# A new placing of stage 1, of the DMA transpositions and of the vector work in a hand-ordered FFT filter and MLP kernel

## The chip, the core and the metric

The kernel runs on one core of a Trainium2 chip. The metric is the device time of one execution in microseconds, as the median of several runs. TensorE (PE) multiplies matrices, with PEld its weight loads; VectorE (DVE), ScalarE (ACT) and GpSimd (POOL) work on elements; SyncE (SP) and POOL issue DMAs. Each engine works through its own instructions in the order in which the program gives them, and waits on semaphores for the others.

## The reference

Eight batches of 3008 tokens with 256 features go through a Fourier filter along the tokens, and every token then through two matrix products with a leaky ReLU between them.

```python
X = np.fft.rfft(x, axis=1)                    # x: (8, 3008, 256)
Y = X * (filt_r + 1j * filt_i)[None, :, :]    # filters: (1505, 256)
y = np.fft.irfft(Y, n=3008, axis=1).astype(np.float32)
h = y.reshape(24064, 256) @ w_in              # w_in: (256, 2048)
out = np.maximum(0.01 * h, h) @ w_out         # w_out: (2048, 256)
```

## The kernel before

**The filter** is a Fourier transform of 3008 = 94 x 32 points, done as small matrix products in fp16. For batches 1 to 7 it has four stages, cut into groups:

- Stage 1 (`s1_group`, 16 groups of a batch, matmuls L265): transforms of length 94. The result is copied out of PSUM into `turn_in` (L266, by ScalarE or VectorE). When all 16 groups are there, six DMA transpositions (`t1_load`, L273, issued by SP) turn `turn_in` into the quads `z1[0]` to `z1[5]`. There is one `turn_in`: the next batch's stage 1 may write it only after the last of the six has read it.
- Stage 2 (`s2_group`, 12 groups, L311): transforms of length 32, then the product with the filter. VectorE makes p2 (L320) and p1 (L323) out of PSUM, SP moves the halves of p2 across partitions with two shift copies (L321, L322), and POOL adds p1 and the shifted p3 to `y` (L326). In the even groups of batch 1 VectorE makes p3 itself (L317, L318), with no shift copies.
- Stage 3 (`sa_group`, 12 groups, L333): the inverse transform of length 32; ScalarE copies the result out (L335), and SP stores it to DRAM (L337). SP loads it back in another order as `z2` (`t2_load`, L281).
- Stage 4 (`sb_group`, 16 groups, L358): the inverse transform of length 94, copied to the ring `yt` (L347), which holds six chunks of 512 tokens.

Batch 0 goes through a separate sequence of steps, written out by hand, at the start.

**The MLP** runs over 47 chunks of 512 tokens. `moe1` (L524) multiplies by `w_in`, 16 tiles to a chunk in pairs into two wide PSUM banks, and ScalarE applies the leaky ReLU (L527, 8 times a chunk) into `gt_c`. The second product (L597) uses, from chunk 3 on, a two-by-two scheme with seven products in place of eight (m1 to m7, among them `last_product`), for which VectorE makes four sums (`act_sums`, L563) and combines the results (L625, L633, L641, L647, L650, L661). SP stores the rows (L583).

**The order** is written by a planner in this file. `at(time, f)` puts the emission of some instructions on a heap, and the heap's order is the program's order on every engine. The times are in units of their own: `SL = 8` units are one chunk. `moe1`, the products and the sums have fixed places in each chunk (`SUMS` for the four sums). The groups of the filter get their places from `PLANS`: for each of batches 1, 2, 3 and 4 (later batches repeat the last row, 47 units on) it has the start and the step of stage 1, the start and the step of stage 2, the lag of stage 3 behind stage 2, the start and the step of stage 4, and the offset and the step of the loads of the next batch's x. No two groups stand closer than `GAP = 0.6` units. A loop over a queue then moves a group back until what it needs has been placed:

- `load_time` places a batch's transpositions `LEAD[0]` units ahead of its stage 2, at the earliest `TURN` after its last stage-1 group, one every `TURNS`.
- A stage-1 group stands at the earliest some units behind the previous batch's last transposition (the line with `TURNS + 0.3`).
- A stage-2 group stands `TURNED` behind its transposition, a stage-4 group `READ` behind its load of z2; a batch's first z2 loads stand `LANDED` behind the last store of stage 3 at the earliest, else `LEAD[1]` ahead of stage 4. Where a place is pushed back, 0.03 is added.

`AFTER` and the numbers in `y_delay` say how far behind stage 2 the shift copies and the additions are emitted (`AFTER[1]`, `AFTER[2]`, `AFTER[3]`), and how far behind a copy the stores (`AFTER[4]`, `AFTER[5]`). `REST` places six late groups of batch 0's inverse transform.

The groups of the filter share two PSUM banks (pf0, pf1; for the first eight units four). `bank` gives a group the one that the planner holds to be free first; `hold` is how long it counts a bank as taken.

Of the kernel before, what the change touches and what calls it, by code (L numbers as in the profile page):

```python
# [19 lines left out]
N1, N2 = 94, 32  # L20
# [3 lines left out]
NW = 96  # L24
# [54 lines left out]
def kernel(  # L79
# [9 lines left out]
    nc = tc.nc  # L89
    B, N, D = x.shape  # L90
# [6 lines left out]
    NCHUNK = TOK // CH  # L97
# [4 lines left out]
    W0 = 3  # L102
    GAP = 0.6
    EXG = 0
    LANDED = 2.43
    READ = 2.2
    TURN = 0.7
    TURNED = 2.2
    TURNS = 0.9
    SUMS = (0.09, 1.59, 2.35, 4)  # L110
    REST = (5.37, 14.61, 8.86, 10.48, 23.53, 20.72)
    DUE = (3.52, 0.66)
    TWICE = (2.2, 2.35)
    LEAD = (3.3, 7.37)
    AFTER = (0.53, 0.8, 1.33, 3.17, 0.39, 0.52)


    PLANS = (
# [4 lines left out]
    )  # L123

    f2_np, i1_np, small_np, i1t_np = _build_np_constants(N)
# [2 lines left out]
    small_d = nc.inline_tensor(small_np, name="small_const")  # L128
# [5 lines left out]
    small_sb = cpool.tile([P, 5, P], FP16, name="small_sb")  # L134
# [29 lines left out]
    def bank(kind, n, w, hold=0.75):  # L164
        if kind == "ph":
            t = wide[turn[kind] % 2]
            turn[kind] += 1
        else:
            i = min(range(len(single)), key=lambda i: frees[i])
            t, frees[i] = single[i], max(frees[i], clock["now"]) + hold  # L170
        return t[:, : n * w].rearrange("p (n w) -> p n w", n=n)
# [12 lines left out]
    def need(*what):  # L184
        for w in what:
            assert w in issued, w

    def noted(what, f):
        f()
        issued.add(what)  # L190

    def soon(delay, f):
        at(clock["now"] + delay, f)
# [24 lines left out]

    EARLY = 6
    x_early = big[1][:].bitcast(FP32)[:, : EARLY * D].rearrange("p (n d) -> p n d", n=EARLY)  # L220
    nc.sync.dma_start(small_sb[:], small_d.ap())
    nc.sync.dma_start(x_early[:R1], bass.AP(tensor=x.tensor, offset=x.offset, ap=[[N2 * D, R1], [D, EARLY], [1, D]]))
    for n0, nn in ((6, 10), (16, 10), (26, 6)):
        x_load(0, n0, nn)
    for i in range(2):
# [32 lines left out]
    def s1_group(b, g, copy):  # L258
        h, dt = divmod(g, 2)

        def go():
            ps = bank("pf", 4, NW)
            need(("x", b, h if b > 1 else 0), *[("z1", b - 1, 5)] * (b > 1))
            for j in range(4):
                nc.tensor.matmul(ps[:, j, :], x_sb[:, 4 * h + j, ts(dt, P)], fwd1m[:, :NW], start=True, stop=True)  # L265
            copy(turn_in[:, :, dt, :, ds(4 * h, 4)], ps.rearrange("p n (q k) -> p k q n", q=4))  # L266
            issued.add(("s1", b, g))
        return go
# [31 lines left out]
    ys = {}  # L300

    def y_delay(b, g):
        return 1.2 if b == 1 and g % 2 == EXG else AFTER[2] if b > 1 else AFTER[3]

    def s2_group(b, g):
        def go():
            ps = bank("pf", 2, D, 1.75 if b == 1 and g % 2 == EXG else 1.2)
            need(("z1", b, g // 2))
            issued.add(("s2", b, g))
            for j in range(2):  # L310
                nc.tensor.matmul(ps[:, j, :], f2_sb[:, 2 * g + j, :],  # L311
                                 z1[g // 2][:, 2 * (g % 2) + j, :],
                                 start=True, stop=True)
            fa, fb = fa_sb[:, ds(2 * g, 2), :], fb_sb[:, ds(2 * g, 2), :]
            p1, p2, p3 = (scrp.tile([P, 2, D], FP32, tag=f"p{i}", name=f"p{i}_b{b}_g{g}") for i in (1, 2, 3))
            if b == 1 and g % 2 == EXG:
                nc.vector.tensor_tensor(p3[0:64], ps[64:P], fb[64:P], AL.mult)  # L317
                nc.vector.tensor_tensor(p3[64:P], ps[0:64], fb[0:64], AL.mult)  # L318
            else:
                nc.vector.tensor_tensor(p2[:], ps, fb, AL.mult)  # L320
                soon(AFTER[1], lambda: nc.sync.dma_start(p3[0:64], p2[64:P]))  # L321
                soon(AFTER[1], lambda: nc.sync.dma_start(p3[64:P], p2[0:64]))  # L322
            nc.vector.tensor_tensor(p1[:], ps, fa, AL.mult)  # L323
            ys[(b, g)] = y1 = ypp.tile([P, 2, D], FP16, tag="y", name=f"y_b{b}_g{g}")
            soon(y_delay(b, g), lambda: noted(
                ("y", b, g), lambda: nc.gpsimd.tensor_tensor(y1[:], p1[:], p3[:], AL.add)))  # L326
        return go

    def sa_group(b, g):
        def go():  # L330
# [5 lines left out]
            if g % 2:  # L336
                soon(AFTER[4], lambda: noted(("st2", b, h), lambda: nc.sync.dma_start(  # L337
                    dz2[b % 2][ds(4 * h, 4)].rearrange("k p d -> p k d"), st2[h % 3])))
# [11 lines left out]
    def sb_group(b, g, copy):  # L350
        h, dt = g // 2, g % 2

        def go():
            ps = bank("pf", 4, NW)[:, :, :N1]
            need(("z2", b, h), ("i1t",))
            issued.add(("sb", b, g))
            for j in range(4):
                nc.tensor.matmul(ps[:, j, :], z2[h % 3][:, j, ts(dt, P)], i1_sb[:, 4 * h + j, :N1],  # L358
                                 start=True, stop=True)
            quad_copy(b, h, dt, ps, copy)  # L360
        return go
# [154 lines left out]
    def moe1(ci, ct):  # L516
# [9 lines left out]
        if j == 1:  # L526
# [15 lines left out]
    LAST = ((-2.9, 1, 0, NCH), (-1.2, 0, 0, NCH // 2), (-0.5, 2, 0, NCH // 2),  # L542
            (1.05, 0, NCH // 2, NCH // 2), (1.1, 2, NCH // 2, NCH // 2), (1.2, 3, 0, NCH // 2), (3.02, 3, NCH // 2, NCH // 2))
# [69 lines left out]
    def stores(ci, i, of=range(2)):  # L613
        for j in of:
            store(ci, 2 * i + j, rows(ci, i)[:, j, 0:2, :].rearrange("p k d -> p (k d)"))
# [7 lines left out]
    def last_product(ci):  # L623
        def after(po):
            add(rows(ci, 0)[:, :, 1], po, rows(ci, 1)[:, :, 2], AL.add)  # L625
            soon(AFTER[5], lambda: stores(ci, 0))
        return product(ci, lambda: sum_places(ci)[3], b22, after, 3)

    def products(ci):
        a11, a12, a21, a22 = (lambda i=i, j=j: quarter(ci, i, j) for i in range(2) for j in range(2))  # L630

        def after5(po):
            add(rows(ci, 1)[:, :, 1:3], twice(po), part[1], AL.add)  # L633
            soon(AFTER[5], lambda: stores(ci, 1))

# [63 lines left out]
    for g in range(10, 16):  # L699
        at(REST[g - 10], lambda g=g: late_sb(1, g - 8, (act, dve)[g < 12 and g % 2]))  # L700

# [33 lines left out]
    def load_time(stage, b, c):  # L735

        end = stage, b, 15 if stage == 1 else 11
        if (stage, b, c) not in loads:
            if stage == 1:
                if end not in when or (b > 1 and (2, b - 1, 2 * c + 1) not in when):  # L740
                    return None
                t = max(first_use[1, b] - LEAD[0], when[end] + TURN) + TURNS * c
                loads[1, b, c] = t = max(t, place.get((1, c), 0))
            else:
                if end not in when or (c > 2 and (4, b, 2 * c - 5) not in when):
                    return None
                loads[3, b, c] = t = max(first_use[3, b] - LEAD[1], place.get((3, c % 3), 0), when[end] + AFTER[4] + LANDED)
            at(t, (t1_load if stage == 1 else t2_load)(b, c))
# [4 lines left out]
    while queue:  # L753
        time, n, stage, b, g, f = heapq.heappop(queue)
        t = max(time, last + GAP)
        if stage == 3:
            behind = when[2, b, g] + y_delay(b, g) + 0.02 if (2, b, g) in when else None
        else:
            behind = load_time(stage - 1, b, g // 2) if stage != 1 else 0
            if stage == 1 and b > 1:  # L760
                behind = load_time(1, b - 1, 5)
                behind = None if behind is None else behind + TURNS + 0.3
            if stage != 1 and behind is not None:
                behind += TURNED if stage == 2 else READ
        if behind is None or behind + 0.02 > t:
            heapq.heappush(queue, (t + GAP if behind is None else behind + 0.03, n, stage, b, g, f))
            continue
        when[stage, b, g] = last = t
        at(t, f)
        if stage in (2, 4) and g % 2:  # L770
            place[stage - 1, g // 2 % (6 if stage == 2 else 3)] = t + 0.1
        assert stage < 4 or t < SL * (QT * (8 * b + g // 2) // CH), (b, g, t)

    for ci in range(NCHUNK + 1):
        if ci < NCHUNK:
            for ct in range(NCT):
                at(SL * ci + 0.5 * ct, lambda ci=ci, ct=ct: moe1(ci, ct))
        if ci == 0:
            continue
        wino = W0 <= ci - 1  # L780
        items = products(ci - 1) if wino else plain(ci - 1)
        for i, f in enumerate(items):
            at(SL * (ci + i / len(items)) + 0.01, f)
        if wino:
            for time, *what in [(v, i) for i, v in enumerate(SUMS)] if ci < NCHUNK else LAST:
                at(SL * ci + time, lambda ci=ci, what=what: act_sums(ci - 1, *what))
    while work:
        clock["now"], _, f = heapq.heappop(work)
# [31 lines left out]
```

## Time and profile before

| what | value |
|---|---|
| median of 3 runs | 752.54 us (751.26 to 752.71) |
| the profiled execution | 753.01 us, of it 751.0 in the span of the profile |
| PE busy | 734.5 us (98%) |
| ACT busy | 549.2 us (73%) |
| DVE busy | 509.7 us (68%) |
| POOL busy | 166.4 us (22%) |
| matmuls | 8129 |
| mean granted TensorE clock | 0.995 |
| DMA | 98.44 MB, 131 GB/s on average |

The span runs from the first instruction to the end of the last. A row of the profile gives the engine, the line of the kernel, what it writes and reads by the program's names, how often, and the busy time. An idle stretch is given with the engine or the DMA whose signal ended it. `big` is a set of buffers that holds `turn_in`, the quads and the sums, so `DMA big<-big` is a DMA transposition, `dz<-big` a store of stage 3 and `big<-dz` a load of z2.

### The profile page before, as it was taken

Reading aid. Unit: us, or ns where it says so; the run is one execution under the profiler, and the core shown is the slowest. Engines: PE = TensorE matmul, PEld = TensorE weight load, DVE = VectorE, ACT = ScalarE, POOL = GpSimd, SP = SyncE. Lnnn points to the kernel's source line nnn. Section 1 sums busy time; section 2 is a strip of 40 time slices with the busy share of each in tenths; the row PEclk is TensorE's granted clock in tenths of the full one; section 3 lists DMA queues with packets and bytes.
Section 4 is the critical chain, followed back from the end, with each engine's and each line's share of the span. In section 5 each row is a group of like instructions: output and inputs, shape, how many; then the busy total and the mean of one; then the engine's idle time right before and its main releaser. Section 6 shows DMA issues by size and latency. Waiting matters only on the chain.

```text
span 751.0 us, 19526 instructions
## 1 busy us (share of the span) xinstructions
PE 734.5 (98%) x8129; PEld 523.9 (70%) x8129; DVE 509.7 (68%) x696; ACT 549.2 (73%) x763; POOL 166.4 (22%) x171
## 2 busy tenths in 40 slices
PE   8999998999899999999999999999999999999997
PEld 3566675776677777777777777777677777777776
DVE  7878556777566676677666767776577676556466
ACT  4775785787687877787788777877777777776762
POOL 5505401232222312222132331212122210000000
PEclk9999999999999999999999999999999999999999
DMA  9967758676856496465865558343664442212012
GB/s 206 222 106 166 186 127 168 145 177 141 186 135 145 120 176 159 116 146 128 166 150 135 134 140 185 99 130 100 122 174 117 109 111 90 63 54 65 29 46 69
DMA packets 128473, 98.44 MB, mean 131 GB/s; under 512 B 59152, under 2 KB 107152, under 8 KB 128192
## 3 DMA queue, kind: packets, MB, share of 16 engines
q1 hardware_dynamic: 113049, 79.51, 41.2%
q0 software_dynamic: 15056, 17.50, 15.9%
q8 instruction: 63, 1.03, 0.6%
q10 hardware_dynamic: 279, 0.19, 0.1%
q14 instruction: 26, 0.21, 0.1%
HBM read 45.97 MB, written 35.65 MB: 109 GB/s over the span
## 4 chain that ended last, share of the span: by engine, by line
PE 91%; DMA 4%; DVE 2%; ACT 1%; SPq 1%; issue 1%; POOL 0%; ACTq 0%; DVEq 0%; POOLq 0%
PE ph L524 42%; PE po_ps L597 18%; PE pf L597 18%; PE pf L265 3%; PE pf L311 2%; PE pf L333 2%; PE pf L358 2%; DMA big<-big 1%; PE pf L689 1%; PE po_ps L689 1%; DMA f_sb<-fwd_const 1%; DMA x_sb<-in_x_dram 1%; DVE big L563 1%; PE pf L432 0%; ACT yt L347 0%
## 5 line engine op out<-in xcount | busy, mean ns | idle before, releaser
L527 ACT ACTIVATE gt_c<-ph 128x1024 f16<-128x1024 f32 x376 | 384.9, 1024 | 133.0 <-PE ph L524 124.2
L524 PE MATMUL ph<-yt,w_in_sb 128*128 128x512 f16 x1504 | 448.8, 380 | 3.4 <-ACT gt_c L527 3.1
L597 PEld LDWEIGHTS <-gt_c 128*128 128x128 f16 x2800 | 201.7, 98 | 99.2 <-issue 1.7
L326 POOL TENSOR_TENSOR y_b_g<-p_b_g,p_b_g 128x512 f16<-128x512 f32 x84 | 116.8, 1392 | 437.1 <-DMA p_b_g<-p_b_g 292.8
L597 PEld LDWEIGHTS <-big 128*128 128x128 f16 x2128 | 151.6, 98 | 66.0 <-issue 0.5
L524 PEld LDWEIGHTS <-w_in_sb 128*128 128x128 f16 x1504 | 118.4, 98 | 9.2 <-issue 3.5
L320 DVE TENSOR_TENSOR p_b_g<-pf,fb_sb 128x512 f32<-128x512 f32 x78 | 53.6, 687 | 33.1 <-PE pf L311 23.5
L597 PE MATMUL po_ps<-wt_sb,gt_c 128*128 128x128 f16 x704 | 69.8, 219 | 0.0
L347 ACT CAST yt<-pf 128x376 f16<-128x376 f32 (+9 forms) x136 | 58.2, 441 | 14.7 <-PE pf L358 11.8
L597 PE MATMUL pf<-w_out_sb,gt_c 128*128 128x128 f16 x720 | 68.5, 221 | 0.0
L597 PE MATMUL pf<-wt_sb,gt_c 128*128 128x128 f16 x688 | 68.1, 219 | 0.0
L597 PE MATMUL pf<-wt_sb,big 128*128 128x128 f16 x704 | 67.9, 219 | 0.0
L597 PE MATMUL po_ps<-wt_sb,big 128*128 128x128 f16 x688 | 65.7, 219 | 0.0
L597 PE MATMUL po_ps<-w_out_sb,gt_c 128*128 128x128 f16 x688 | 65.0, 219 | 0.0
L563 DVE TENSOR_TENSOR big<-gt_c 128x2048 f16<-128x2048 f16 (+1 forms) x46 | 56.8, 1235 | 3.4 <-ACT gt_c L527 3.3
L563 DVE TENSOR_TENSOR big<-big,gt_c 128x2048 f16<-128x2048 f16 (+1 forms) x45 | 57.4, 1275 | 0.1
L323 DVE TENSOR_TENSOR p_b_g<-pf,fa_sb 128x512 f32<-128x512 f32 x84 | 57.2, 681 | 0.2
L563 DVE TENSOR_TENSOR big<-gt_c,big 128x2048 f16<-128x2048 f16 (+1 forms) x45 | 56.9, 1264 | 0.0
L563 DVE TENSOR_TENSOR gt_c<-gt_c 128x2048 f16<-128x2048 f16 x43 | 56.0, 1303 | 0.9
L335 ACT CAST big<-pf 128x512 f16<-128x512 f32 x84 | 49.0, 584 | 10.4 <-PE pf L333 8.2
L266 ACT CAST big<-pf 128x384 f16<-128x384 f32 x90 | 42.8, 476 | 16.5 <-DMA big<-big 8.1
L358 PE MATMUL pf<-i_sb,big 128*128 128x94 f16 x448 | 37.1, 207 | 0.0
(98 smaller groups left out, 644.9 us busy)
## 6 DMA issues: line engine op xcount, KB each, us to landing
p_b_g<-p_b_g SPq DMA_DIRECT2D x156, 128.0 KB
out_dram<-ost_c_h SPq DMA_DIRECT2D x118, 128.0 KB
dz<-big SPq DMA_DIRECT2D x42, 256.0 KB
big<-dz SPq DMA_DIRECT2D x56, 192.0 KB
x_sb<-in_x_dram POOLq DMA_DIRECT2D x40, 192.0 KB, 4.2
x_sb<-in_x_dram POOLq DMA_DIRECT2D x2, 768.0 KB, 8.8
w_in_sb<-in_moe_w_in_dram POOLq DMA_DIRECT2D x1, 1024.0 KB, 12.8
w_out_sb<-in_moe_w_out_dram POOLq DMA_DIRECT2D x1, 1024.0 KB, 13.7
```

The costliest lines, as they stand in the source:

```text
L265: nc.tensor.matmul(ps[:, j, :], x_sb[:, 4 * h + j, ts(dt, P)], fwd1m[:, :NW], start=True, stop=True)
L266: copy(turn_in[:, :, dt, :, ds(4 * h, 4)], ps.rearrange("p n (q k) -> p k q n", q=4))
L320: nc.vector.tensor_tensor(p2[:], ps, fb, AL.mult)
L323: nc.vector.tensor_tensor(p1[:], ps, fa, AL.mult)
L326: ("y", b, g), lambda: nc.gpsimd.tensor_tensor(y1[:], p1[:], p3[:], AL.add)))
L335: nc.scalar.copy(st2[h % 3][:, ds(2 * (g % 2), 2), :], ps)
L347: copy(yt[:, dt, ds(to, 4 * n)].rearrange("p (a c) -> p a c", c=4), v[:, ds(a, n)])
L358: nc.tensor.matmul(ps[:, j, :], z2[h % 3][:, j, ts(dt, P)], i1_sb[:, 4 * h + j, :N1], start=True, stop=True)
L524: nc.tensor.matmul(ph[:, j, :], w_in_sb[:, dt, ts(ct, P)], yt[:, dt, ds(ci * CH % RING, CH)], start=(dt == 0), stop=(dt == NDT - 1))
L527: nc.scalar.activation(gts[ci][:, ds(2 * g, 2), :], ph, AF.Lrelu)
L563: nc.vector.tensor_tensor(*(v[:, ds(c0, n)] for v in (o, i0, i1)), op)
L597: nc.tensor.matmul(of[t], a()[:, c, ts(t, P)], w[:, c, :], start=(c == 0), stop=(c == NCH - 1))
```

## The change

Nothing is computed otherwise; only places in the order and two DMAs at the start are changed.

- The distance of a batch's first stage-1 groups behind the previous batch's last transposition gets a number of its own, `MARGIN`: 3.838 units in place of `TURNS + 0.3` = 1.2.
- Transpositions start 3.9 instead of 3.3 units ahead of stage 2 and stand 1.015 instead of 0.9 apart.
- `PLANS` is changed for all batches, among it stage 1 of batch 1, 3 and 4 and later, the lag of stage 3 in batch 4 and later, and the loads of x.
- The sums of each chunk stand at other places, with a separate list (`SUMS_FIRST`) for chunk 3; the additions (`AFTER`, `y_delay`), the stores and the late groups of batch 0 (`REST`) move.
- Banks count as held for 0.432 units by groups of stages 1 and 4 (before 0.75) and for 0.753 by groups of stage 2 (before 1.2).
- At the start `small_sb` is loaded in two DMAs: its first fifth (`fwd1`) ahead of `x_early`, the rest behind it.

```diff
-    LANDED = 2.43
-    READ = 2.2
-    TURN = 0.7
-    TURNED = 2.2
-    TURNS = 0.9
-    SUMS = (0.09, 1.59, 2.35, 4)
-    REST = (5.37, 14.61, 8.86, 10.48, 23.53, 20.72)
+    LANDED = 2.836
+    READ = 1.712
+    TURN = 0.889
+    TURNED = 2.3
+    TURNS = 1.015
+    MARGIN = 3.838
+    YD = (0.966, 1.75, 0.753, 0.432, 1.2)
+    SUMS_FIRST = (0.018, 2.103, 2.35, 4)
+    SUMS = (0.322, 1.569, 2.418, 4)
+    REST = (5.339, 14.69, 8.396, 11.015, 24.419, 20.72)
...
-    LEAD = (3.3, 7.37)
-    AFTER = (0.53, 0.8, 1.33, 3.17, 0.39, 0.52)
+    LEAD = (3.9, 7.293)
+    AFTER = (0.454, 0.757, 1.245, 2.615, 0.39, 0.731)
...
-        (0.68, 0.31, 12.6, 1.05, 4.3, 38.33, 2.78, 7.78, 1.5),
-        (23.6, 0.8, 42.87, 2.62, 7.4, 85.59, 2.85, 7.0, 2.12),
-        (46.5, 1.6, 77.28, 3.57, 5.62, 130.03, 2.65, 1.5, 2.2),
-        (79.5, 2.2, 119.86, 3.87, 7.04, 177.42, 2.92, 1.5, 2.55),
+        (0.01, 0.254, 12.6, 1.065, 4.3, 35.584, 2.78, 8.122, 1.518),
+        (23.983, 0.737, 42.87, 2.58, 7.4, 85.174, 2.85, 2.756, 2.12),
+        (47.4, 1.5, 77.28, 3.57, 5.62, 130.659, 2.547, 1.5, 1.552),
+        (81.42, 2.0, 119.86, 3.87, 6.302, 177.538, 2.92, 1.5, 2.55),
...
-    nc.sync.dma_start(small_sb[:], small_d.ap())
+    nc.sync.dma_start(small_sb[:, 0], small_d.ap()[:, 0])
     nc.sync.dma_start(x_early[:R1], ...)
+    nc.sync.dma_start(small_sb[:, 1:], small_d.ap()[:, 1:])
...
-            ps = bank("pf", 4, NW)
+            ps = bank("pf", 4, NW, YD[3])
...
-        return 1.2 if b == 1 and g % 2 == EXG else AFTER[2] if b > 1 else AFTER[3]
+        return YD[0] if b == 1 and g % 2 == EXG else AFTER[2] if b > 1 else AFTER[3]
...
-            ps = bank("pf", 2, D, 1.75 if b == 1 and g % 2 == EXG else 1.2)
+            ps = bank("pf", 2, D, YD[1] if b == 1 and g % 2 == EXG else YD[2])
...
-                behind = None if behind is None else behind + TURNS + 0.3
+                behind = None if behind is None else behind + MARGIN
...
-            for time, *what in [(v, i) for i, v in enumerate(SUMS)] if ci < NCHUNK else LAST:
+            for time, *what in [(v, i) for i, v in enumerate(SUMS if ci - 1 > W0 else SUMS_FIRST)] if ci < NCHUNK else LAST:
```

More of the change, by code (lines that the diff above doesn't have):

```diff
@@ L353, in go @@
         def go():
-            ps = bank("pf", 4, NW)[:, :, :N1]
+            ps = bank("pf", 4, NW, YD[3])[:, :, :N1]
             need(("z2", b, h), ("i1t",))
```

## The prediction

> **What bounds the kernel now.** I read the page first, then the list of TensorE's waits, then the order of time around the two longest of them, then the granted clock there, and last the queue of SyncE (SP) that issues the DMA transpositions.
>
> The page says that TensorE is the bound:
>
> ```profile
> span 751.0 us, 19526 instructions
> PE 734.5 (98%) x8129; PEld 523.9 (70%) x8129; DVE 509.7 (68%) x696; ACT 549.2 (73%) x763; POOL 166.4 (22%) x171
> ```
>
> So a change of order alone, which neither adds nor removes a matmul, can only win what TensorE spends idle or at a low clock. TensorE's own waits, longest first (us in total, times, longest):
>
> ```profile
> PE ph L524 <- ACT gt_c L527: 3.1, 1, 3.1
> PE pf L311 <- ACT big L266: 2.7, 1, 2.7
> ...
> PE pf L333 <- DVE p_b_g L323: 0.7, 1, 0.7
> ...
> PE pf L311 <- DMA big<-big: 0.4, 1, 0.4
> ...
> PE pf L265 <- ACT big L335: 0.3, 1, 0.3
> ```
>
> The two long ones are single events, at 126 us and at 196 us. Both have one cause, seen in ScalarE's order of time (start, us, instruction, idle before it):
>
> ```profile
> 127.64 0.48 ACT L266 CAST big<-pf 128x384 f16<-128x384 f32 x1 [4.70 <-DMA big<-big]
> ...
> 197.89 0.48 ACT L266 CAST big<-pf 128x384 f16<-128x384 f32 x1 [3.43 <-DMA big<-big]
> ```
>
> L266 is the eviction of the next batch's first stage-1 group into turn_in. It may not write before the previous batch's last DMA transposition has read turn_in. ScalarE works in order, so the evictions behind it (gt_c, and a yt of the inverse stage) wait too, and TensorE runs out of PSUM banks. The windows show a second loss (PE, PEld, DVE, ACT, POOL busy, then granted clock):
>
> ```profile
> 131.00:132.00 1.00, 1.00 (x10) 0.88 (x9) 1.00 (x2) 0.95 (x1) 0.42 (x1) 0.50 0.85 244
> 132.00:133.00 1.00, 1.00 (x7) 0.45 (x5) 1.00 (x3) 0.08 (x1) 0.00 (x0) 0.50 0.87 90
> ...
> 199.00:200.00 1.00, 1.00 (x7) 0.48 (x5) 0.99 (x2) 0.67 (x1) 0.71 (x1) 0.50 0.95 288
> 200.00:201.00 1.00, 1.00 (x8) 0.72 (x7) 1.00 (x2) 0.37 (x1) 1.00 (x2) 0.50 0.16 46
> ```
>
> After each gap the clock is halved for a while. With the neighbouring microseconds (0.64 and 0.66 at 130 and 133; 0.77 and 0.52 at 198 and 201) the first stretch loses 0.36 + 0.50 + 0.50 + 0.34 = 1.70 us, the second 0.23 + 0.50 + 0.50 + 0.48 = 1.71 us.
>
> Why the transposition was late, in SP's order of time:
>
> ```profile
> 120.77 1.32 SPq L273 DMA_TRANSPOSE big<-big  x1
> 122.20 0.53 SPq L321 DMA_DIRECT2D p_b_g<-p_b_g  x1
> 122.77 0.60 SPq L322 DMA_DIRECT2D p_b_g<-p_b_g  x1
> 123.42 2.26 SPq L273 DMA_TRANSPOSE big<-big  x1
> 125.77 0.53 SPq L281 DMA_DIRECT2D big<-dz  x1
> ```
>
> SP is issue-bound there: one follows the other with no pause, 1.3 us a transposition, 0.5 to 0.8 us a copy or store. The chain of waits puts the landing 4.09 us behind the issue at 123.42, at 127.50.
>
> **The change part by part.** Only the order on each engine counts; a planned place is a sort key. Eight units are one chunk. From 200 to 550 us the trace has 186 evictions L527, 8 to a chunk, so a chunk takes 350 / 186 x 8 = 15.05 us and a unit 1.88 us.
>
> *The margin.* I worked the planner's placing loop through with both sets of numbers. The last transposition of batch 2 stands at 42.87 - 3.3 + 5 x 0.9 = 44.07 before and 42.87 - 3.9 + 5 x 1.015 = 44.05 after. Batch 3's first group stood at 46.50; now 44.05 + 3.838 pushes it to 47.91: 1.41 units or 2.65 us later. Batch 3 to 4: the last transposition at 78.48 and 78.45, the first group at 79.71 (78.48 + 1.2 + 0.03) and 82.32 (78.45 + 3.838 + 0.03): 2.61 units, 4.9 us. For the other batches the margin never binds (7.4 units or more are there). So it acts at exactly the two places of the two stalls.
>
> *First stall.* In SP's new order the first transposition of batch 2 stands before a 0.31 us load, the second before a store, and one z2 load (0.53 us) goes ahead of the last transposition. Adding the rows up (1.33 us a transposition, 0.8 a store, 0.6 a copy) I get it issued near 123.6 again, so it lands at 127.0 to 128.2. TensorE's matmuls for the group, at 123.16 before, come at 123.16 + 2.65 = 125.8; ScalarE has one more gt_c eviction ahead of it and reaches it at 126.7. It waits 0.3 to 1.5 us instead of 4.70. Two wide banks gave 4.70 - 3.15 = 1.55 us of cover before, so TensorE waits 0 to 1 us; I take 0.4. Win: 3.15 + 1.70 - 0.4 = 4.45 us.
>
> *Second stall.* The same sum puts the last transposition of batch 3 at 194.1 (two shift copies now before it) and its landing near 197.3; the eviction comes at 193.40 + 4.9 + 0.33 = 198.6. It no longer waits. Win: 2.70 + 1.71 = 4.41 us. If that cover of 1.3 us were gone, the cost would return in steps up to these 4.41.
>
> [...]
>
> *Third wait, 0.69 us at 172.75.* A stage-3 group (L333) waited for a bank that L323 emptied late, behind VectorE's sums L563 of 2.31 and 1.96 us. Stage-2 group 9 of batch 2 was placed at 68.05, after the sum at 68.00; now it is at 67.71, ahead of it. Win 0.69; bounds 0 and 0.69.
>
> *Small ones.* The 0.38 us at 538 (batch 7's stage 2 waiting for its first transposition) goes: that transposition is 0.6 units or 1.1 us earlier and now ahead of two shift copies. A 0.13 us gap at 79.39 goes, as the late inverse group moves from 0.13 to 0.96 units behind the user of its bank. The 0.35 us at 83.22 is half kept: the group takes another bank, which VectorE empties at 83.27 instead of ScalarE's 83.52. Win together 0.38 + 0.13 + 0.17 = 0.68.
>
> *Lag 7.04 to 6.302 (batches 4 to 7).* Stage 3 comes 0.74 units or 1.39 us sooner after stage 2. Between the end of the addition L326 and the matmul L333 the trace leaves 0.05 us at batch 7's first group (a wait of 0.20 already), 1.68 at batch 4's, 1.9 at batch 6's, 3.1 at batch 5's. Only batch 7's is short, and its shift copies also issue about 1.3 us earlier in the new SP order. Cost 0 to 1.2 us; I take 0.3.
>
> *Additions, sums, banks.* Additions L326 (AFTER, YD) move by up to 0.56 units on POOL, which is 22% busy; sum 0 moves by 0.23 units, still 6.6 units ahead of its product; shorter holds change which of two banks a group takes, but the least reuse distances stay (0.6 and 1.2 units). Queued behind an early addition or an x load on POOL are only other additions. Batch 4's x loads now follow their stage-1 groups by 0.06 to 1 unit; they wait a little, and nothing reads them for 10 units. The z2 loads (LANDED, READ, LEAD) move by half a unit at most against their stage 4; the trace leaves 4.1 us or more between the end of a batch's first load issue and its first L358, so nothing there. Cost -0.3 to +0.8, taken as 0.3 for waits I have not seen.
>
> *Start.* x_early (L222) no longer has 128 KB of small_sb before it. At some 250 GB/s this is 0.5 us, and ScalarE waited 3.64 us for x_early. But the chain then runs over the x_sb loads and the last third of f2_sb (landing at 20.03), whose bytes are unchanged. Stage 1 of batch 1 starts 0.65 units sooner, where its x is just landing (issue 26.44 + 8.8 gives 35.2 to 35.9; needed at 36.0). Bounds -0.4 and +0.6; taken as 0.
>
> Sum: 4.45 + 4.41 + 0.69 + 0.68 - 0.3 - 0.3 = 9.6 us. TensorE is busy without a gap from 200 to 400 us, so what is won earlier stays won. The profiled execution took 753.01 us (span 751.0) and is 0.47 above the median 752.54: profiled 743.4, median 742.9.
>
> **Rivals.**
> *One stall stays or a new one takes its place.* SP's backlog decides: if the last transposition lands 2 us later than summed, ScalarE again holds back gt_c and one gap with its half clock returns, 4.4 us: 747.3. For it: batch 2's six transpositions, planned over 5 x 0.9 units = 8.5 us, were issued from 111.10 to 123.42, 3.9 us behind the plan. Against: the new order spreads the transpositions and starts them sooner. Chance 0.13.
> *The clock loss is a matter of phase.* If the half clock follows such gaps only in some executions, the median gains only the idle times: 752.54 - 9.6 + 3.4 = 746.3. Against: two gaps of two had it. [...] Chance 0.05.
> *Nothing moves.* The eviction waits for something else than the transposition, and the gap moves with it. The releaser in both rows is the transposition, so 0.05; 752.5.
> *Slower: stage 3 now waits for the additions.* In batches 4 to 7 the lag loses 1.39 us. If shift copies land 2.5 us later than now, the first stage-3 group of each of the four waits about 2.7 us and brings the half clock, 4 x (2.7 + 1.7) = 17.6 us, so 752.5 - 9.6 + 17.6 = 760.5. It decides from 2.4 us a batch on, clock included. For it: 0.05 us of slack at batch 7. Against: 1.7 to 3.1 us at the other three. Chance 0.09.
>
> **How the numbers follow.** The forecast, both stalls gone, has 0.68 and gives 742.9; its own range is 740.9 (11.6: all interior gaps, 7.8, the clock, 3.4, and the start's 0.4, at no cost) to 745. The first two rivals are taken into the range: 741 to 748.5, which leaves out no more than 2 in 10. About 0.2% (1.5 us) is what a measurement of this kernel can tell from no change. Faster: 0.68 + 0.13 + 0.05 = 0.86, less 0.01 for cases near 751, 0.85; same 0.06; slower 0.09.
>
> **What would show it.** Right: no wait of TensorE above 1 us after 36 us, granted clock 1.00 in every stretch there, ScalarE's L266 waiting for the transposition under 1.6 us, TensorE's busy time some 3.4 us lower (the half clock's share), the third wait gone. Wrong: a wait of L333 for L326 in batches 4 to 7, or a clock of 0.50 at a new place; a transposition of batch 2 or 3 landing over 2 us later than 127.5 or 197.8 would refute the SP sum.

## The result, and the profile after

The changed kernel takes 741.05 us (median of 4 runs, 740.08 to 741.88), the kernel before, on the same chip, 751.9 us (4 runs, 750.27 to 752.71). The ratio is 0.9862, with a 95% interval of 0.984 to 0.9883: a win of 8.8 to 12.0 us. The forecast was 742.9 in 741 to 748.5, so the median lies at the lower edge of the range. The profiled execution took 741.42 us, 11.6 less than that of before.

The head of the page after:

```profile
span 739.5 us, 19530 instructions
PE 730.3 (99%) x8129; PEld 521.7 (71%) x8129; DVE 510.1 (69%) x696; ACT 550.0 (74%) x763; POOL 169.0 (23%) x171
```

The same 8129 matmuls keep TensorE busy for 4.2 us less; 3.4 us of that is work that no longer runs at half clock (1.70 and 1.71 us), and no run shows what makes up the rest. The other 7.3 us of the span were idle time. In the list of TensorE's waits after (us in total, times, longest) neither of the two long ones, nor the third wait at L333, is left:

```profile
PE po_ps L384 <- DVE one L242: 1.2, 1, 1.2
PE pf L337 <- POOL y_b_g L330: 1.2, 1, 1.2
PE ph L390 <- ACT x_sb L477: 0.5, 1, 0.5
```

L384 and L390 belong to the first microseconds. L337 is stage 3 (L333 before; the new file is four lines longer); its 1.18 us stand at 537.6, at the first stage-3 group of batch 7. ScalarE's first evictions of the next batch's stage 1 (start, us, instruction, idle before it), the rows that waited 4.70 and 3.43 us before:

```profile
125.44 0.48 ACT L270 CAST big<-pf 128x384 f16<-128x384 f32 x1 [0.29 <-DVE ost_c_h L637]
...
191.66 0.48 ACT L270 CAST big<-pf 128x384 f16<-128x384 f32 x1 [0.69 <-DMA big<-big]
```

The first finds the transposition landed, the second waits 0.69 us for it, which the banks cover. The windows around both places (length, then PE, PEld, DVE, ACT, POOL busy, then granted clock, DMA share, GB/s) show a full TensorE at full clock:

```profile
120.00:130.00 10.00, 10.00 (x117) 7.25 (x116) 7.27 (x11) 7.62 (x11) 3.61 (x3) 1.00 0.96 187
...
190.00:200.00 10.00, 10.00 (x121) 7.24 (x119) 7.05 (x10) 8.09 (x14) 2.21 (x3) 1.00 0.73 188
```

SP's order of time after, for the last two transpositions of batch 2:

```profile
117.91 1.32 SPq L277 DMA_TRANSPOSE big<-big  x1
119.34 0.53 SPq L325 DMA_DIRECT2D p_b_g<-p_b_g  x1
119.91 0.60 SPq L326 DMA_DIRECT2D p_b_g<-p_b_g  x1
120.61 0.53 SPq L285 DMA_DIRECT2D big<-dz  x1
121.19 2.20 SPq L277 DMA_TRANSPOSE big<-big  x1
```

One z2 load now goes ahead of the last transposition, as worked out; the queue is still issue-bound.

Where the 11.5 us of span come from is read by setting the same eviction of moe1 (L527, L531 after) in both traces side by side. The changed kernel leads by 0.6 us at 36.8 (time of before), 1.3 at 114.8, 6.3 at 148, 7.2 at 176, 11.9 at 208, 11.75 at 515, 11.3 at 580 and 11.5 at the end. So: 0.6 at the start, 0.7 in small gaps, 5.0 at the first stall, 0.9 at the third wait, 4.7 at the second stall, nothing for 300 us, and 0.4 lost on balance in batch 7.

### The profile page after: what moved, and what is told of

It reads as the page before. It is cut to its first block, busy times and chain, and to the rows that moved or that the text cites. A ratio compares the mean times of both kernels' runs of the same rounds, so it can differ in the third digit from the quotient of the medians.

```text
span 739.5 us, 19530 instructions
## 1 busy us (share of the span) xinstructions
PE 730.3 (99%) x8129; PEld 521.7 (71%) x8129; DVE 510.1 (69%) x696; ACT 550.0 (74%) x763; POOL 169.0 (23%) x171
## 4 chain that ended last, share of the span: by engine, by line
PE 92%; DMA 3%; POOL 1%; ACT 1%; SPq 1%; DVE 1%; issue 0%; POOLq 0%
PE ph L528 43%; PE pf L601 18%; PE po_ps L601 18%; PE pf L362 3%; PE pf L269 2%; PE pf L315 2%; PE pf L337 2%; DMA fa_sb<-in_filt_r_dram 1%; PE pf L693 1%; PE po_ps L693 1%; DMA fa_sb<-in_filt_i_dram 1%; DMA p_b_g<-p_b_g 1%; SPq L277 1%; POOL prod L416 0%; ACT yt L351 0%
## 5 line engine op out<-in xcount | busy, mean ns | idle before, releaser
L531 ACT ACTIVATE gt_c<-ph 128x1024 f16<-128x1024 f32 x376 | 385.5, 1025 | 132.4 <-PE ph L528 125.4
L330 POOL TENSOR_TENSOR y_b_g<-p_b_g,p_b_g 128x512 f16<-128x512 f32 x84 | 119.2, 1420 | 421.1 <-DMA p_b_g<-p_b_g 292.9
L601 PE MATMUL po_ps<-wt_sb,gt_c 128*128 128x128 f16 x704 | 71.8, 219 | 0.0
L270 ACT CAST big<-pf 128x384 f16<-128x384 f32 x90 | 43.0, 479 | 10.9 <-PE pf L269 8.8
```

The source lines that it names most:

```text
L531: nc.scalar.activation(gts[ci][:, ds(2 * g, 2), :], ph, AF.Lrelu)
L601: nc.tensor.matmul(of[t], a()[:, c, ts(t, P)], w[:, c, :], start=(c == 0), stop=(c == NCH - 1))
```

## The experiments

All were run against the kernel before on the same chip (medians of before there 750.3 to 751.3); ratios have 95% intervals. Three questions: is it the distance alone, what does the rest of the change do, and what is the wait in batch 7 worth?

**The distance alone.** Before, with one number changed:

```diff
-                behind = None if behind is None else behind + TURNS + 0.3
+                behind = None if behind is None else behind + 3.838
```

> The kernel before with one number changed: a stage-1 group stands 3.838 units, not TURNS + 0.3 = 1.2, behind the previous batch's last transposition. By the planner's arithmetic this puts the first groups of batches 3 and 4 at 47.94 and 82.35 (before 46.50 and 79.71; in the changed kernel 47.91 and 82.32) and moves little else. Theory A, the two stalls are only a matter of this distance: both gaps (3.15 and 2.70 us) and both half-clock stretches (1.70 us each) go, 751.9 - 9.3 = 742.6 us, TensorE's wait at 172.75 (0.69 us) may stay or go. Theory B, the earlier and wider placed transpositions on SP are needed as well: the first stall stays in part (a gap of 1 to 2 us, perhaps with its half clock), 744.5 to 748 us.

Measured: 745.58 us (744.24 to 746.66), ratio 0.9936 (0.9917 to 0.9956). Both stalls and both half clocks are gone (mean granted clock 0.999 in the profiled execution, 0.995 in before): the evictions wait 1.64 and 0.66 us, and 0.31 us of idle TensorE is left at 129. Yet only about half of the win is there. The time is that of the second theory, but not for its reason: the first stall is gone. New waits stand at the second place, in the list of TensorE's waits:

```profile
PE pf L358 <- DMA big<-dz: 1.6, 1, 1.6
...
PE pf L333 <- POOL y_b_g L326: 0.8, 2, 0.6
```

Stage 3 waits for an addition, stage 4 for a load of z2. Both wait for things that SP issues behind batch 3's transpositions; its order of time:

```profile
183.41 8.02 SPq L273 DMA_TRANSPOSE big<-big  x5
191.53 1.24 SPq L321 DMA_DIRECT2D p_b_g<-p_b_g  x1
192.82 0.58 SPq L322 DMA_DIRECT2D p_b_g<-p_b_g  x1
193.50 0.54 SPq L337 DMA_DIRECT2D dz<-big  x1
...
197.84 1.50 SPq L281 DMA_DIRECT2D big<-dz  x3
```

Five transpositions in one train, then the shift copies that the addition needs, then the store that the z2 load needs. The reading is that they had time to catch up while TensorE stood still for 2.7 us. A new wait in the stall's place is what the prediction's first rival said, though from another queue entry than it named.

**The changed kernel without the distance.** The loads of x keep their places, so only the stage-1 groups of batches 3 to 7 move back:

```diff
-    MARGIN = 3.838
+    MARGIN = 1.2
-        (47.4, 1.5, 77.28, 3.57, 5.62, 130.659, 2.547, 1.5, 1.552),
-        (81.42, 2.0, 119.86, 3.87, 6.302, 177.538, 2.92, 1.5, 2.55),
+        (46.5, 1.5, 77.28, 3.57, 5.62, 130.659, 2.547, 2.4, 1.552),
+        (79.5, 2.0, 119.86, 3.87, 6.302, 177.538, 2.92, 3.42, 2.55),
```

> The changed kernel with the distance alone undone: MARGIN 1.2, stage 1 of batches 3 and 4 starting at 46.5 and 79.5 as before (their x loads keep their absolute places). The first groups then stand at 46.50 and 79.69, while everything else of the change stays. Theory A: both stalls come back, with their half clock: 741.05 + 9.2 = 750 us. Theory B, the new order on SP brings the transpositions earlier: the gaps come back smaller, 1 to 2 us each, 743.5 to 747 us. If neither comes back (741 to 742), the win was in something else.

Measured: 747.74 us (745.11 to 751.13, 12 runs), ratio 0.9973 (0.9953 to 0.9992). This lies between the two theories: the second stall is back in full, the first in part. The list of its waits has

```profile
PE pf L269 <- ACT big L270: 4.0, 2, 2.7
```

with gaps of 1.34 and 0.60 us at 124 to 126 and of 2.69 at 191.5, the latter alone with the half clock (0.50 from 195 to 197; 1.00 from 124 to 128). Against the change's 0.9862, taking the distance away costs 0.0111, or 8.3 us; against its second measurement further down, 0.9892, it costs 0.0081, or 6.1 us. To the kernel before the distance adds 4.8 us (0.0064 x 751). That the distance and the rest need each other is shown by the new waits in the traces; the times alone would not settle it.

**A shorter distance.** Before with 3.0 in place of 3.838, executed once:

```diff
-                behind = None if behind is None else behind + TURNS + 0.3
+                behind = None if behind is None else behind + 3.0
```

> The kernel before with 3.0 units instead of 1.2: batch 4's first group at 81.51 (no wait), batch 3's at 47.10, only 0.6 units or 1.1 us later than before. Theory A, the eviction's wait shrinks by what the group is moved: ScalarE waits some 3.6 us, TensorE some 2.0 us. On the clock: if a gap of 2 us is enough for the half clock, 3.4 us of it follow the gap and the time is 751.9 - 4.4 - 1.1 = 746.4 us; if not, 744.7 us and no stretch under 1.00. Theory B, the gap jumps (other evictions come between): TensorE waits under 1 us and the time is 743 to 744 us.

Measured: 748.08 us, once. Gaps of 1.05 and 0.32 us at 126 to 128, and a new one of 2.52 at 194.2, where L333 waits for the addition. The mean granted clock of 0.998 is worth about one half clock (0.002 x 746 = 1.5 us) and does not tell where it stood. The expectation missed the second place: there the limit is again the shift copies, not the transposition.

**Distance and spacing.** Is it the wider spacing of the transpositions that clears SP's queue? Before, with the distance and

```diff
-    TURNS = 0.9
+    TURNS = 1.015
-    LEAD = (3.3, 7.37)
+    LEAD = (3.9, 7.37)
```

> The kernel before with the distance of 3.838 units and the transpositions placed as in the changed kernel (3.9 instead of 3.3 units ahead of stage 2, 1.015 instead of 0.9 apart). With the distance alone both gaps were gone, but 2.2 us came back at 196 to 202 us: L333 waited 0.60 us for an addition and L358 1.60 us for a z2 load, both queued on SP behind five transpositions in a row. Theory B, that backlog is what the wider spacing takes away: the two waits fall to 0 to 0.7 us together and the time by 1.5 to 2.2 us below the distance alone, ratio 0.990 to 0.992. Theory C, the backlog comes from the shift copies of batch 3, which stay behind the last transposition here and stand ahead of it in the changed kernel: the waits stay at 1.5 to 2.2 us, ratio 0.993 to 0.994.

Measured: 745.41 us, ratio 0.9935 (0.9916 to 0.9953); run again

> The kernel before with distance and spacing once more, as the measure for the swap on the same chip: 745 to 745.5 us, and a wait of L333 for L326 of 1 to 2.5 us near 193 us in its profile.

745.46 us, 0.994 (0.9918 to 0.9961). The same as with the distance alone: the spacing does not clear it. In the first profile nothing is left at the first place and the wait at the second is longer, with a clock of 0.50 from 196 to 198:

```profile
195.65 0.58 PE L333 MATMUL pf<-y_b_g,small_sb 128*128 128x512 f16 x1 [2.28 <-POOL y_b_g L326]
```

In the second profile TensorE waits at two places, 0.95 us at L333 and 2.46 at L358, with no half clock (1.00 from 194 to 205).

**The spacing alone**, the same two numbers at the old distance of 1.2:

> The kernel before with the transpositions placed as in the changed kernel and the distance kept at 1.2 units (first groups of batches 3 and 4 at 46.50 and 79.69, as before). Theory A, the distance is what counts: both gaps stay, the first at 2 to 3.2 us (the last transposition of batch 2 comes 1 us sooner at most), the second at 2.5 to 3 us, ratio 0.996 to 1.000. Theory B, the spacing alone does half of it: ratio 0.992 to 0.995.

Measured: 749.6 us (12 runs), ratio 0.9988 (0.9973 to 1.0003): no difference that can be told. Gaps of 2.29 us at 124.2 and 2.38 at 192.8, both with their half clock (0.50 from 128 to 131, 0.51 from 196 to 199).

**Shift copies ahead of the last transposition.** In the changed kernel two shift copies of batch 3's first stage-2 group stand ahead of the last transposition. This does that alone, on top of distance and spacing:

```diff
-                soon(AFTER[1], lambda: nc.sync.dma_start(p3[0:64], p2[64:P]))
-                soon(AFTER[1], lambda: nc.sync.dma_start(p3[64:P], p2[0:64]))
+                soon(0.55 if (b, g) == (3, 0) else AFTER[1], lambda: nc.sync.dma_start(p3[0:64], p2[64:P]))
+                soon(0.55 if (b, g) == (3, 0) else AFTER[1], lambda: nc.sync.dma_start(p3[64:P], p2[0:64]))
```

> The kernel before with the distance of 3.838 units and the wider spacing (as in the run with both), and one swap on SP: the two shift copies of batch 3's first stage-2 group stand ahead of batch 3's last transposition, where the changed kernel has them, not behind it. No other engine's order differs. Theory C, the late shift copies are what came in place of the second stall (L333 waited 2.28 us for the addition at 193 to 196 us, and the half clock followed): the copies issue 1.2 to 2 us sooner, the wait falls to under 1 us without the half clock, and the last transposition, 1.2 us later, still lands before its eviction is due or holds it up by less than 2 us. Time 742.5 to 743.5, 2 to 3 us under the run with both. Theory D, the wait is that of POOL or of DMA traffic: it stays at 2 us or more and the time does too.

Measured: 746.0 us, ratio 0.994 (0.9921 to 0.996). The wait for the addition falls to 0.14 us, as expected, and the time does not move: L358 now waits 2.16 us for z2. One wait hid the next. (Three of the six executions have a mean granted clock of 0.997 or 0.998, the profiled one 0.999, so the median may hold a half clock that this profile does not show.) SP's order of time there:

```profile
183.41 5.29 SPq L273 DMA_TRANSPOSE big<-big  x3
188.81 0.54 SPq L321 DMA_DIRECT2D p_b_g<-p_b_g  x1
```

Three transpositions take 5.29 us to issue; the changed kernel's row for the same three has 4.02. On POOL a load of x for batch 4 is issued just then, and another one just ahead of the z2 loads that L358 waits for:

```profile
183.46 0.54 POOL L204 DMA_DIRECT2D x_sb<-in_x_dram  x1
...
194.56 0.54 POOL L204 DMA_DIRECT2D x_sb<-in_x_dram  x1
...
196.12 1.60 SPq L281 DMA_DIRECT2D big<-dz  x3
...
200.56 0.34 PE L358 MATMUL pf<-i_sb,big 128*128 128x94 f16 x4 [2.16 <-DMA big<-dz]
```

**That, and batch 4's loads of x out of the way**, at the places of the changed kernel:

```diff
-        (46.5, 1.6, 77.28, 3.57, 5.62, 130.03, 2.65, 1.5, 2.2),
+        (46.5, 1.6, 77.28, 3.57, 5.62, 130.03, 2.65, 2.4, 1.552),
```

> The kernel before with distance, spacing and the swap on SP, and batch 4's x loads 1.552 instead of 2.2 units apart (starting at 48.9 in place of 48.0, the changed kernel's places): the last two, which ran at 183 and 194 us beside the transpositions and the z2 loads, go ahead of the transpositions. The wait left in the run with the swap was L358's for the first z2 load (2.16 us at 198 us). Theory E, DMA traffic beside the transpositions delays the chain behind them (stage-3 store, z2 loads): the wait falls to under 1.2 us and the time by 1 to 2 us (ratio 0.991 to 0.992). Theory F, it is the place of the last stage-3 group of batch 2 and of its store: the wait stays at 1.8 us or more.

Measured: 742.23 us (741.76 to 746.24), ratio 0.9896 (0.9866 to 0.9926). In the profile:

```profile
186.71 4.02 SPq L273 DMA_TRANSPOSE big<-big  x3
...
192.10 2.52 SPq L273 DMA_TRANSPOSE big<-big  x1
...
199.04 1.45 SPq L281 DMA_DIRECT2D big<-dz  x3
...
202.08 0.34 PE L358 MATMUL pf<-i_sb,big 128*128 128x94 f16 x4 [0.95 <-DMA big<-dz]
```

and the wait for z2 is 0.95 us. No load of x is issued between 176.1 and 200 there; in the changed kernel none between 176.8 and 196.6. The ratio falls by 0.0044, some 3.3 us; the two intervals, each against the kernel before on its own chip, overlap by 0.0005. The profiled execution is the slowest of the six, 746.24 us: it had lost 2.8 us by its first moe1 eviction (39.25 against 36.47 in the run with the swap), and its mean granted clock is 0.996, that of the five others 0.999 or 1.000.

What became shorter is not SP's queue. The three transpositions are issued in 4.02 instead of 5.29 us, but the fourth takes 2.52 instead of 1.62, with no load of x near. A transposition of over 2 us stands elsewhere too without such a load (2.26 us at 123.42 in before), so a load that delays SP is not shown. This trace runs 2.75 us behind the other there (the moe1 evictions at 190.87 and 193.62), and the z2 loads are issued 2.92 later, so no sooner. But from their issue to L358 it is 3.04 us here and was 4.44 with a load of x issued 1.56 us ahead. In the two other profiles in which L358 waited over 1 us for z2, a load of x also stood 0.3 to 1 us ahead, and it took 4.19 us (distance alone) and 5.71 (second profile of distance and spacing). So in these traces the z2 loads land later beside a load of x; that is Theory E, but for the part of the transpositions in it.

With distance, spacing, the swap and the x loads the ratio is 0.9896, against 0.9862 and 0.9892 in the two measurements of the whole change. By the medians all other parts together bring 0.3 to 2.6 us, with intervals that overlap; of these parts only the two below were run by themselves.

**Or an earlier stage 3**, in place of the x loads, by batch 2's stage-2 step as in the change:

```diff
-        (23.6, 0.8, 42.87, 2.62, 7.4, 85.59, 2.85, 7.0, 2.12),
+        (23.6, 0.8, 42.87, 2.58, 7.4, 85.59, 2.85, 7.0, 2.12),
```

> The kernel before with distance, spacing and the swap on SP, and batch 2's stage 2 in steps of 2.58 instead of 2.62 units, as in the changed kernel: its last stage-2 group stands at 73.11 instead of 73.71 and its last stage-3 store, which the first z2 loads wait for, at 79.04 instead of 79.48, 0.44 units or 0.83 us sooner. Theory F: L358's wait for the z2 load (2.16 us in the run with the swap) falls by 0.8 us or, with the shift copies of that group now ahead of the second transposition, to 0 to 1.3 us; ratio 0.991 to 0.993. Theory E, traffic: the wait stays near 2 us.

Measured: 745.02 us, ratio 0.992 (0.9892 to 0.9949). The wait for z2 is gone, so an earlier stage 3 removes it too, but 0.70 us at 158.5 and 0.87 us at L333 at 204.1 have come. The 1 us against the run without it lies within the intervals: no verdict on the time.

**The lag.** The changed kernel with the old lag of 7.04 in batches 4 to 7:

```diff
-        (81.42, 2.0, 119.86, 3.87, 6.302, 177.538, 2.92, 1.5, 2.55),
+        (81.42, 2.0, 119.86, 3.87, 7.04, 177.538, 2.92, 1.5, 2.55),
```

> The changed kernel with the lag of stage 3 behind stage 2 in batches 4 to 7 at 7.04 units again instead of 6.302. Theory A, TensorE's one wait left (1.18 us at 537.6, for the addition L326 of batch 7's first group) is the 1.39 us that the shorter lag took away: the wait falls to 0 to 0.2 us and the time to 739.9 to 740.1 us. Theory B, the addition itself is late (it took 2.26 us there instead of 1.27) and the wait stays or moves: 741 us and a wait of about 1 us.

Measured: 742.34 us, ratio 0.9895 (0.9877 to 0.9914). Batch 7's wait falls from 1.18 to 0.20 us, but batch 6 has a new one:

```profile
453.59 0.38 PE L337 MATMUL pf<-y_b_g,small_sb 128*128 128x512 f16 x1 [1.06 <-POOL y_b_g L330]
```

and there are 0.55 and 0.45 us at 192 and 197. The old lag everywhere is no better.

**The old lag in batch 7 alone**, and the change itself once more on the same chip:

```diff
-        plan(b, p[0] + z, p[1], p[2] + z, p[3], p[4], p[5] + z, *p[6:])
+        plan(b, p[0] + z, p[1], p[2] + z, p[3], p[4] + (0.74 if b == 7 else 0), p[5] + z, *p[6:])
```

> The changed kernel with the lag of stage 3 at 7.04 units in batch 7 alone, 6.302 kept in batches 4 to 6. The wait of 1.18 us at batch 7's first group was 1.18 in both kernels with the shorter lag and 0.2 in all four with the longer one. Theory A, it is the lag: 0.2 us there, nothing new elsewhere, 0.9 to 1.0 us less than the changed kernel (740.1 against 741.05, or 0.13%, at the edge of what the times can tell). Theory B, waiting work is only put off: another wait of about 1 us follows within batch 7 and the times are the same.

> The changed kernel once more, on the chip of this call, so that the others of this call can be set beside it: 741 us, ratio 0.985 to 0.988, one wait of TensorE above 1 us (L337 at batch 7's first group, 1.2 us). If the small waits at 190 to 200 us differ from the first profile, where there were none, they are a matter of the single execution.

Measured: 740.4 us (739.93 to 741.97), ratio 0.9876 (0.9856 to 0.9895), against 741.57 (741.43 to 743.23), 0.9892 (0.9873 to 0.9912) for the change. The wait of 1.18 us stands again at 537.7 in the change, and in the other its row in the list of TensorE's waits is

```profile
PE pf L337 <- POOL y_b_g L330: 0.2, 1, 0.2
```

with no gap above 0.2 us from 36 us on. The medians differ by 1.2 us, the size of that wait, but the intervals overlap: the wait is shown, the time only likely. Its median is the lowest of all runs, but its ratio lies within the intervals of both measurements of the change.

## Why the prediction was right, point by point

- **What bounds it.** Right: TensorE's idle time fell by 7.3 us and its busy time by 4.2 (summed: 3.4 from the half clock).
- **The margin binds at two places only.** Right: with 1.2 again gaps come back at these two places and 6.1 to 8.3 us of the win are gone. Put in alone, though, the distance brings 4.8 us and not the 8.9 of the two stalls; see the first rival.
- **First stall, 4.45 us.** Measured 5.0. The sum for SP was off: the last transposition was issued at 121.19, or 122.5 in before's time (1.3 us lead), 1.1 us earlier than the summed 123.6. The eviction no longer waits for it, and the 0.4 us kept for TensorE are not seen.
- **Second stall, 4.41 us.** Measured 4.7, but the cover was mis-sized. The issue was summed at 194.1 and came at 187.16 + 6.95 (the lead there) = 194.1. The landing was put 3.2 us behind it and came at 191.66, 4.5 behind; ScalarE reached the eviction 0.7 us sooner than summed. The cover of 1.3 us became a wait of 0.69, against the forecast that ScalarE would not wait at all. The win came even so because the banks took it, which was not counted on here; with the swap they took 1.97 us at this eviction without a gap.
- **Third wait, 0.69 us.** The wait is gone and the lead grows by 0.9 there.
- **Small ones, 0.68 us.** The lead gained 0.7 before the first stall and the wait for batch 7's first transposition went. No run takes these apart.
- **Lag, 0.3 us of 0 to 1.2.** Mis-sized: the wait came where it was named, at batch 7's first group, at 1.18 us, the upper end. Batch 7 had 0.20 us of wait before, so about 1.0 us is the lag's. A wait of L333 for L326 in batches 4 to 7 stood among the prediction's signs of being wrong, and one wait above 1 us among what a right one would not show: both came, for this one term.
- **Start, 0.** No difference shown. The first L527 stands at 35.2 to 39.3 us in the profiles without the split load of small_sb and at 35.8 to 36.6 with it; one profile's 0.6 us is no more than that spread.
- **Unforeseen waits, 0.3 us.** None above 0.2 us but batch 7's.
- **The sum of 9.6 us** against 10.9 in the medians of the same chip and 11.5 in the spans. Of the 1.9 us more in the spans 0.8 are the two stalls (5.0 + 4.7 for 4.45 + 4.41), 0.6 the start, 0.4 the small gaps before the first stall (0.7 for 0.30), 0.2 the third wait and 0.3 the unforeseen waits that did not come; batch 7 goes the other way by 0.5 (0.4 lost where 0.08 was to be won). Nearly all errors lie on one side, which is why the median came out at the edge of the range.
- **First rival.** It did not happen in the change, and it is what happens when the distance alone is put in. The prediction had priced the distance on the transpositions' landing and taken the z2 loads behind them as harmless, with "4.1 us or more" of room between the end of a first load's issue and its L358. That was not free room: from the start of the issue the z2 loads take 3.04 to 5.71 us to the matmul that waits for them. In the changed order no wait came of it. Copies ahead of the last transposition and x loads out of the stretch bring the kernel before with distance and spacing to 742.23 us; batch 2's earlier stage 2 was run only in place of the x loads. Which of them counts most is not settled beyond the x loads' 3.3 us.
- **Second rival, the clock's phase.** Its time of 746.3 did not come, but it is partly true of the kernel before. Among the executions of the kernel before beside the run with the distance alone, those with a mean granted clock of 0.995 or less have a median span of 749.3 us, those with 0.997 or more 746.9. That is what one or both half clocks (1.7 us each) missing from some executions would give; only the profiled ones show where they were.
- **The slower rival.** Fell: batches 4 to 6 show no wait at L337, batch 7 one of 1.18 us without a half clock (1.00 from 531 to 545).

## What to carry to other kernels

When a stall is a writer kept out of a buffer by the last reader, moving the writer's place behind the reader is worth the whole gap and what follows it; but the same stall gave every other queue time to catch up, so list what those queues issue next and who reads it, and move that first. A change of one place that brings half of what its stall costs has met the next wait: look at the same microseconds again before giving it up. A load that nothing needs yet, issued just ahead of one that is waited for, can lengthen the other's landing (4.2 to 5.7 us against 3.0 here): look at the queues of all engines, not only at the one that issues.

## What the runs showed of the hardware

**In these traces the length of a gap alone does not tell whether a half clock follows it.** Inside before there are two half-clock stretches, 130.28 to 133.69 and 198.54 to 201.95, each 3.41 us at a granted clock of 0.50, behind gaps of TensorE of 3.15 and 2.70 us. A clock of 0.50 or 0.51 also stands behind the gaps of 2.69 us (distance undone, 195 to 197), of 2.29 and 2.38 us (spacing alone, 128 to 131 and 196 to 199) and of 2.28 us (first profile of distance and spacing, 196 to 198). No half clock follows 1.18 us (the changed kernel, 1.00 from 531 to 545), 1.60 us (distance alone, 1.00 from 194 to 204), 2.16 us (shift copies first, 1.00 from 193 to 203) or 2.46 us (second profile of distance and spacing, 1.00 from 194 to 205). So a gap of 2.28 us cost a half clock and one of 2.46 us cost none; what decides between them is not shown.
